# Turning 64-bit weights into float32: the exponent's shift of range moved into ScalarE's absolute value

## The chip, the cores and the metric

The kernel runs on one core of one Trainium2 chip. The core has TensorE (PE in the profile) for matrix products, VectorE (DVE), ScalarE (ACT), GpSimd (POOL) and SyncE (SP), whose queue issues most transfers. Each engine works through a queue of its own in order and waits on semaphores for the others. The metric is the device time of one execution in microseconds (us), from the median of several runs.

## What is computed

```python
# attention, per batch and head: x 512x64, state 32x64, in float32
xread = softmax(x @ state.T / 8) @ state
sread = softmax(state @ x.T / 8) @ x
# rows of both, concatenated: 4352 tokens of 512
...
h = x @ w_in                    # 512 -> 2048
g = np.maximum(h, 0.0) + np.log1p(np.exp(-np.abs(h)))
x = g @ w_out                   # 2048 -> 512
...
# a router gives every token to one of 8 experts, at most 544 each
out[mask] = np.maximum(x[mask] @ w1[e], 0.0) @ w2[e]
```

The weights `w_in` (512 x 2048) and `w_out` (2048 x 512) arrive as 64-bit floats. The chip's engines have no such type, so the kernel reads them as pairs of 32-bit integers, a low and a high word, and makes float32 numbers of them by bit operations. This is called turning the weights below.

## The kernel before

The program goes through attention and the first layer batch by batch (8 batches; the first product of the layer, then softplus, then the second product), then the routing, then the experts one after the other. Float32 products are made of three products of shorter parts: a matrix is split into `hi` (rounded, by ScalarE) and `lo` (what is left, by GpSimd or VectorE), and `hi*hi`, `hi*lo`, `lo*hi` are added up in PSUM.

The weights are turned while batch 0 is worked on. There are 32 units of 128 partitions x 512 numbers: 16 of `w_in` ("i") and 16 of `w_out` ("o"), in an order written out by hand (`queue`). A unit goes through these steps:

- `conv_load`: SyncE loads 512 KB of integers into a buffer `st64` (four of them).
- `conv_abs` (L181): ScalarE takes the absolute value of the high words, read as float32, into `c_a` (three of them).
- `conv_steps`, on VectorE: L196 raises it to at least 2^-15; L198 shifts it left by three and masks it; L200 joins sign and top exponent bit from the high word; L208 joins the three top bits of the low word, into `win` for an "i" unit, into a buffer `c_f` (four of them) for an "o" unit.
- `conv_post`, for an "o" unit: TensorE turns `c_f` (L232) into `p_bg`, ScalarE copies it to `wt` (L234) and rounds `c_f` into `wo_hi` (L238), and GpSimd makes `wo_lo` (L239).

`conv_steps` is a generator. Each `yield` ends a step, and `fill(n)`, called between other work, advances the units in progress by n steps; with two in progress it takes them in turn. A unit that ends starts the next load.

The work around it is written out by hand in rounds, one for each of the 16 column blocks `ft` of batch 0, as words in the strings `play0`; for the last seven rounds (9 to 15):

```python
play0 += ["g main main fill4 first a p att fill2 abs log abs second post fill2"] * 7
```

`first` is the first product of round s+2 (L493, six matmuls into `p_h`), `a` and `log` are ScalarE's parts of softplus (`t_sp`, L528, L535, L536), `g` is VectorE's sum for round s+1 (L548) with ScalarE's `g_hi` (L556) and GpSimd's `g_lo` (L559), and `second` is the second product (L577 with `wo_hi`, L579 with `wo_lo`, L581 with `g_lo`; twelve matmuls). `p` makes a pair `P_hi`, `P_lo` from `win` (L441 on TensorE, L427 on ScalarE, L429 on VectorE, with `fill(2)` between), and `att` is one step of the attention of the next batch (L386, L388, L334 and others on VectorE). `main` takes a unit into progress, `abs` is `conv_abs`, `post` is `conv_post`. The PSUM banks `bg0` and `bg1` are shared by all small products; a product into one of them waits until the last reader has finished.

Of the kernel before, what the change touches and what calls it, by code (L numbers as in the profile page):

```python
# [8 lines left out]
F32 = mybir.dt.float32  # L9
# [3 lines left out]
AF = mybir.ActivationFunctionType  # L13
OP = mybir.AluOpType
# [9 lines left out]
NJ4 = -(-NJ // 4) * 4  # L24
NFT = FF // 128
BIG = 3.0e38
TINY = 2.0 ** -15


@with_exitstack  # L30
def attn_moe_kernel(ctx, tc, x_s, x_t, state_t, w_in, w_out, w_gate, w1, w2, out):
    nc = tc.nc
    V, A, G, PE, SP = nc.vector, nc.scalar, nc.gpsimd, nc.tensor, nc.sync
# [141 lines left out]
    def conv_abs():  # L175
        if not loaded or len(ready) == 2:
            return
        u, st = loaded.pop(0)
        w = st.rearrange("p (n two) -> p n two", two=2)
        a = cv.tile([128, 512], F32, name="c_a", bufs=3)  # L180
        A.activation(a, w[:, :, 1].bitcast(F32), AF.Abs)  # L181
        ready.append((u, w[:, :, 0], w[:, :, 1], a))

    cops = []
# [1 line left out]
    def conv_main(n=1):  # L186

        for _ in range(n):
            if ready and not (ready[0][0][0] == "o" and len(turned) + sum(c[0] == "o" for c in cops) == 4):
                u, lo, hi, a = ready.pop(0)  # L190
                f = cv.tile([128, 512], F32, name="c_f", bufs=4) if u[0] == "o" else None
                cops.append((u[0], conv_steps(u, lo, hi, a, f)))

    def conv_steps(u, lo, hi, a, f):
        t = a.bitcast(I32)
        V.tensor_scalar(a, a, TINY, None, op0=OP.max)  # L196
        yield
        V.tensor_scalar(t, t, 3, 0x3FFFFFFF, op0=OP.logical_shift_left, op1=OP.bitwise_and)  # L198
        yield
        V.scalar_tensor_tensor(t, hi, -(1 << 30), t, op0=OP.bitwise_and, op1=OP.bitwise_or)  # L200
        yield
        if u[0] == "o":
            dst = f.bitcast(I32)
            turned.append((f, u[1]))
        else:
            dst = win[:, 2 * u[2]:2 * u[2] + 2, u[1] * 256:(u[1] + 1) * 256].bitcast(I32)
            lo, t = (x.rearrange("p (h c) -> p h c", h=2) for x in (lo, t))
        V.scalar_tensor_tensor(dst, lo, 29, t, op0=OP.logical_shift_right, op1=OP.bitwise_or)  # L208
# [487 lines left out]
    def play(script, s):  # L696
        for w in script.split():
            op, n = w.rstrip("0123456789"), w.lstrip("abcdefghijklmnopqrstuvwxyz")
            if op == "fill":
                fill(int(n))  # L700
            elif op == "att":
                if s < 0 or s in ATT0:
                    att_step(0)
            elif op == "first":
                mlp1(s + 2)
            elif op == "a":
                softplus_abs(s + 2)
            elif op == "g":
                softplus_b(s + 1)
            elif op == "second":  # L710
                mlp2(s)
                ghl.pop(s)
            else:
                {"main": conv_main, "abs": conv_abs, "post": conv_post, "p": p_unit, "log": softplus_log}[op]()
# [552 lines left out]
    for ph in range(E):  # L1267
# [19 lines left out]
        for u in range(16):  # L1287
            ft, hf = units[u] if ph else units0[u]
            f, c = slice(ft * 128, (ft + 1) * 128), HALF[hf]
            w = c.stop - c.start  # L1290
# [115 lines left out]
```

## Time and profile before

| | |
|---|---|
| median of 3 runs | 1197.72 us (1197.44 to 1198.61) |
| the profiled execution's own time | 1192.96 us |
| its span, first to last instruction | 1191.2 us |
| TensorE busy | 1137.9 us, 96% of the span |
| VectorE busy | 654.8 us, 55% |
| ScalarE busy | 640.1 us, 54% |
| GpSimd busy | 485.5 us, 41% |
| mean granted TensorE clock | 0.990 |

Busy time counts an instruction from start to end; matmuls overlap, so a busy TensorE is not one at its peak. The shares are means over stages that differ much from each other. The profiled execution is one run and not the median one, so durations read from it add up to its own time.

### The profile page before, as it was taken

The page shows a single profiled execution, that of the slowest core. Times are in us where ns is not written, and L with a number is a line of the kernel's source. Part 1 is how long each engine was busy: PE and PEld are TensorE (multiplying, and loading weights), DVE is VectorE, ACT ScalarE, POOL GpSimd, SP SyncE. Part 2 cuts the span into 40 slices and gives each one's busy share as a digit, 9 for nine tenths or more (in the row PEclk, how much of TensorE's full clock was granted, in tenths as well). Part 3 has the DMA queues.
Part 4 walks back from the last instruction along what each step waited for, and adds up shares of the span by engine and source line. Part 5 has one row for each costly group of instructions (what it writes and reads, how often), then busy time and mean ns, then how long its engine had stood idle before and what let it go on. Part 6 is the DMA issues. An engine that isn't in the chain of part 4 may idle for free.

```text
span 1191.2 us, 21162 instructions
## 1 busy us (share of the span) xinstructions
PE 1137.9 (96%) x8216; PEld 901.5 (76%) x8216; DVE 654.8 (55%) x1754; ACT 640.1 (54%) x1277; POOL 485.5 (41%) x472
## 2 busy tenths in 40 slices
PE   4898999999999999999999997999999999999996
PEld 1666677777777777777777765979797989889895
DVE  6999536463363533634434267776686858662220
ACT  3776666666676666766776732533333333334340
POOL 0334323233233232323344435645636555547531
PEclk9999999999999999999999999899999999999998
DMA  7464020111201102002000003250523324365401
GB/s 248 143 196 141 1 72 36 54 53 37 71 1 48 60 32 60 16 37 71 1 18 19 1 18 125 92 199 21 207 80 139 126 101 153 103 165 169 129 10 37
DMA packets 56020, 97.99 MB, mean 82 GB/s; under 512 B 5232, under 2 KB 24048, under 8 KB 55920
## 3 DMA queue, kind: packets, MB, share of 16 engines
q1 hardware_dynamic: 50192, 78.69, 20.6%
q0 software_dynamic: 5632, 17.83, 4.4%
q8 instruction: 64, 1.05, 0.4%
q14 instruction: 36, 0.29, 0.1%
q10 hardware_dynamic: 96, 0.13, 0.0%
HBM read 76.58 MB, written 17.83 MB: 79 GB/s over the span
## 4 chain that ended last, share of the span: by engine, by line
PE 80%; DVE 9%; issue 6%; POOL 2%; ACT 1%; DMA 1%; SPq 0%; POOLq 0%; DVEq 0%; ACTq 0%
PE p_h L493 13%; PE p_y L1344 12%; PE p_y L577 9%; PE p_y L579 8%; PE p_y L581 8%; PE p_y L1299 7%; PE p_h L1299 6%; PE p_bg L462 2%; PE p_y L584 2%; PE p_bg L504 2%; PE p_y L588 2%; PE p_y L586 2%; DVE c_a L200 1%; PE p_h L1208 1%; PE p_bg L1047 1%
## 5 line engine op out<-in xcount | busy, mean ns | idle before, releaser
L559 POOL TENSOR_TENSOR g_lo<-g,g_hi 128x512 fp32r<-128x512 f32 x127 | 164.8, 1298 | 318.3 <-ACT g_hi L556 287.5
L577 PE MATMUL p_y<-g_hi,wo_hi 128*128 128x512 f32 x448 | 184.5, 412 | 0.0
L579 PE MATMUL p_y<-g_hi,wo_lo 128*128 128x512 f32 x448 | 176.3, 393 | 3.4 <-POOL wo_lo L239 3.4
L581 PE MATMUL p_y<-g_lo,wo_hi 128*128 128x512 f32 x448 | 176.7, 394 | 0.6 <-POOL g_lo L559 0.6
L556 ACT ACTIVATE g_hi<-g 128x512 fp32r<-128x512 f32 x126 | 79.6, 631 | 115.3 <-DVE g L548 81.2
L548 DVE SCALAR_TENSOR_TENSOR g<-p_h,t_sp 128x512 f32<-128x512 f32 x128 | 87.5, 684 | 98.0 <-ACT t_sp L536 97.3
L577 PEld LDWEIGHTS p_y<-g_hi,wo_hi 128*128 128x128 f32 x448 | 84.8, 189 | 47.5 <-ACT t_sp L528 12.6
L1344 PE MATMUL p_y<-w2h,h2h 128*128 128x512 f32 x256 | 104.1, 406 | 0.0
L493 PE MATMUL p_h<-at_hi,P_hi 128*128 128x512 f32 x256 | 103.1, 403 | 0.0
L1344 PE MATMUL p_y<-w2l,h2h 128*128 128x512 f32 x256 | 101.4, 396 | 0.0
L1344 PE MATMUL p_y<-w2h,h2l 128*128 128x512 f32 x256 | 101.1, 395 | 0.0
L493 PE MATMUL p_h<-at_hi,P_lo 128*128 128x512 f32 x256 | 100.8, 394 | 0.0
L493 PE MATMUL p_h<-at_lo,P_hi 128*128 128x512 f32 x256 | 100.8, 394 | 0.0
L579 PEld LDWEIGHTS p_y<-g_hi,wo_lo 128*128 128x128 f32 x448 | 85.1, 190 | 20.2 <-POOL wo_lo L239 4.6
L581 PEld LDWEIGHTS p_y<-g_lo,wo_hi 128*128 128x128 f32 x448 | 84.7, 189 | 19.7 <-POOL g_lo L559 1.0
L1352 POOL DMA_INDIRECT out_dram<-ot,idx x40 | 38.8, 970 | 136.6 <-ACT ot L1333 69.2
L528 ACT ACTIVATE t_sp<-p_h 128x512 f32<-128x512 f32 x128 | 75.4, 589 | 25.5 <-PE p_h L493 25.5
L1178 POOL TENSOR_TENSOR w2l<-s2w,w2h 128x512 fp32r<-128x512 f32 x64 | 81.7, 1294 | 13.0 <-ACT w2h L1177 12.2
L1178 POOL TENSOR_TENSOR w1l<-s1w,w1h 128x512 fp32r<-128x512 f32 x63 | 80.2, 1300 | 7.8 <-ACT w1h L1177 7.3
L536 ACT ACTIVATE t_sp<-t_sp 128x512 f32<-128x512 f32 x128 | 81.0, 633 | 4.1
L535 ACT ACTIVATE t_sp<-t_sp 128x512 f32<-128x512 f32 x128 | 80.8, 631 | 2.3
L1299 PE MATMUL p_y<-yTl,w1h 128*128 128x288 f32 (+1 forms) x256 | 77.3, 302 | 0.0
(283 smaller groups left out, 2607.7 us busy)
## 6 DMA issues: line engine op xcount, KB each, us to landing
s2w<-in_moe_w_dram SPq DMA_DIRECT2D x8, 2048.0 KB, 9.4
s1w<-in_moe_w_dram SPq DMA_DIRECT2D x6, 2048.0 KB, 8.3
st<-in_moe_w_in_dram SPq DMA_DIRECT2D x16, 512.0 KB, 4.1
xT<-in_x_t_dram SPq DMA_DIRECT2D x16, 512.0 KB, 4.4
st<-in_moe_w_out_dram SPq DMA_DIRECT2D x16, 512.0 KB, 3.5
xt<-in_x_s_dram SPq DMA_DIRECT2D x8, 1024.0 KB, 5.5
y_d<-yz SPq DMA_DIRECT2D x48, 128.0 KB, 3.4
s1w<-in_moe_w_dram SPq DMA_DIRECT2D x8, 512.0 KB, 8.2
```

The source lines that it names most:

```text
L493: PE.matmul(h, l[:, f0:f0 + 128], r[:, par, :], start=(n == 0), stop=(n == 5))
L535: A.activation(t, t, AF.Exp, scale=-1.0)
L536: A.activation(t, t, AF.Ln, bias=1.0)
L548: V.scalar_tensor_tensor(g[:, :w], hps.pop(s)[:, :w], 0.0, tsp.pop(s)[:, :w], op0=OP.max, op1=OP.add)
L556: A.activation(hi[:, c], g[:, c], AF.Copy)
L559: (G if on[1] == "G" else V).tensor_tensor(lo[:, c], g[:, c], hi[:, c].bitcast(F32), op=OP.subtract)
L577: PE.matmul(yb[j], wo_hi[:, ft, c], hi, start=st, stop=False)
L579: PE.matmul(yb[j], wo_lo[:, ft, c], hi, start=False, stop=False)
L581: PE.matmul(yb[j], wo_hi[:, ft, c], lo, start=False, stop=sp)
L1178: eng.tensor_tensor(lo, src, hi.bitcast(F32), op=OP.subtract)
L1299: PE.matmul(p[:, :w], l[:, k, f], r[:, k, c], start=(n == 0), stop=(n == 11))
L1344: PE.matmul(p, l[:, ft, c], r[:, ft, :], start=(n == 0), stop=(n == 23))
```

## The change

The constant 2^-15 goes, and 2^-112 comes. ScalarE's absolute value multiplies by it: a float32's exponent field goes down by 112, so the bits that L198's mask cut off are already zero, and small numbers go to zero by themselves. VectorE's maximum (L196) is left out, and so is the mask of the shift (L198); the sign is now taken alone from the high word, without the exponent's top bit. A unit has three steps where it had four. Behind the edit, line numbers are two lower in the changed kernel: L198, L200 and L208 of before correspond to L196, L198 and L206.

```diff
--- before.py
+++ after.py
@@ -24,7 +24,7 @@
 NJ4 = -(-NJ // 4) * 4
 NFT = FF // 128
 BIG = 3.0e38
-TINY = 2.0 ** -15
+DOWN = 2.0 ** -112
 
 
 @with_exitstack
@@ -178,7 +178,7 @@
         u, st = loaded.pop(0)
         w = st.rearrange("p (n two) -> p n two", two=2)
         a = cv.tile([128, 512], F32, name="c_a", bufs=3)
-        A.activation(a, w[:, :, 1].bitcast(F32), AF.Abs)
+        A.activation(a, w[:, :, 1].bitcast(F32), AF.Abs, scale=DOWN)
         ready.append((u, w[:, :, 0], w[:, :, 1], a))
 
     cops = []
@@ -193,11 +193,9 @@
 
     def conv_steps(u, lo, hi, a, f):
         t = a.bitcast(I32)
-        V.tensor_scalar(a, a, TINY, None, op0=OP.max)
+        V.tensor_scalar(t, t, 3, None, op0=OP.logical_shift_left)
         yield
-        V.tensor_scalar(t, t, 3, 0x3FFFFFFF, op0=OP.logical_shift_left, op1=OP.bitwise_and)
-        yield
-        V.scalar_tensor_tensor(t, hi, -(1 << 30), t, op0=OP.bitwise_and, op1=OP.bitwise_or)
+        V.scalar_tensor_tensor(t, hi, -(1 << 31), t, op0=OP.bitwise_and, op1=OP.bitwise_or)
         yield
         if u[0] == "o":
             dst = f.bitcast(I32)
```

The instructions of TensorE, ScalarE, GpSimd and SyncE are the same and stand in the same order as before. On VectorE, fewer steps for the same `fill` calls change the order too. Two places are shown. In the rows, `c_a` and `st` are the unit in progress, `win` or `c_f` its result, numbers are buffers.

The first is VectorE's queue ahead of the first `g`, near 30 us; before:

```order
L429 TENSOR_TENSOR P_lo<-p_bg_275,P_hi 128x256
L200 SCALAR_TENSOR_TENSOR c_a<-st_204,c_a 128x512
L196 TENSOR_SCALAR c_a<-c_a 128x512
L429 TENSOR_TENSOR P_lo<-p_bg_289,P_hi 128x256
L208 SCALAR_TENSOR_TENSOR win<-st_204,c_a 128x2x256
L196 TENSOR_SCALAR c_a<-c_a 128x512
L198 TENSOR_SCALAR c_a<-c_a 128x512 x2
L548 SCALAR_TENSOR_TENSOR g<-p_h,t_sp 128x512
L200 SCALAR_TENSOR_TENSOR c_a<-st_208,c_a 128x512
L200 SCALAR_TENSOR_TENSOR c_a<-st_242,c_a 128x512
```

and now:

```order
L427 TENSOR_TENSOR P_lo<-p_bg_269,P_hi 128x256
L206 SCALAR_TENSOR_TENSOR win<-st_198,c_a 128x2x256
L196 TENSOR_SCALAR c_a<-c_a 128x512
L427 TENSOR_TENSOR P_lo<-p_bg_283,P_hi 128x256
L198 SCALAR_TENSOR_TENSOR c_a<-st_202,c_a 128x512
L196 TENSOR_SCALAR c_a<-c_a 128x512
L206 SCALAR_TENSOR_TENSOR c_f<-st_202,c_a 128x512
L198 SCALAR_TENSOR_TENSOR c_a<-st_236,c_a 128x512
L546 SCALAR_TENSOR_TENSOR g<-p_h,t_sp 128x512
L206 SCALAR_TENSOR_TENSOR win<-st_236,c_a 128x2x256
```

The first `g` had two joins from a unit's last two lines ahead of it in this piece, and now has four, of three units; the joins that stood behind it moved ahead.

The second is VectorE's queue in round 10, near 109 us, from the two units in progress there to the next `g`; before:

```order
L196 TENSOR_SCALAR c_a<-c_a 128x512 x2
L198 TENSOR_SCALAR c_a<-c_a 128x512 x2
L200 SCALAR_TENSOR_TENSOR c_a<-st_1121,c_a 128x512
L200 SCALAR_TENSOR_TENSOR c_a<-st_1128,c_a 128x512
L429 TENSOR_TENSOR P_lo<-p_bg_1261,P_hi 128x256
L448 COPY Vp<-p_bg_1261 128x8
L386 TENSOR_REDUCE m_1296<-p_bg_1291 128x16
L388 TENSOR_TENSOR P_994<-p_bg_1291,m_1296 128x512
L208 SCALAR_TENSOR_TENSOR c_f<-st_1121,c_a 128x512
L208 SCALAR_TENSOR_TENSOR c_f<-st_1128,c_a 128x512
L548 SCALAR_TENSOR_TENSOR g<-p_h,t_sp 128x512
```

and now:

```order
L196 TENSOR_SCALAR c_a<-c_a 128x512 x2
L198 SCALAR_TENSOR_TENSOR c_a<-st_1092,c_a 128x512
L198 SCALAR_TENSOR_TENSOR c_a<-st_1101,c_a 128x512
L206 SCALAR_TENSOR_TENSOR c_f<-st_1092,c_a 128x512
L206 SCALAR_TENSOR_TENSOR c_f<-st_1101,c_a 128x512
L427 TENSOR_TENSOR P_lo<-p_bg_1232,P_hi 128x256
L446 COPY Vp<-p_bg_1232 128x8
L384 TENSOR_REDUCE m_1267<-p_bg_1262 128x16
L386 TENSOR_TENSOR P_971<-p_bg_1262,m_1267 128x512
L546 SCALAR_TENSOR_TENSOR g<-p_h,t_sp 128x512
```

The two last joins of the units, into `c_f`, moved from behind the attention step (L386, L388, now L384, L386) to ahead of `P_lo`, and two shifts are gone.

## Rows read from the trace of the kernel before

**Rows 1.** The page: engines, then two groups of ScalarE instructions (count, busy us, mean ns).

```profile
PE 1137.9 (96%) x8216; PEld 901.5 (76%) x8216; DVE 654.8 (55%) x1754; ACT 640.1 (54%) x1277; POOL 485.5 (41%) x472
...
L536 ACT ACTIVATE t_sp<-t_sp 128x512 f32<-128x512 f32 x128 | 81.0, 633 | 4.1
L535 ACT ACTIVATE t_sp<-t_sp 128x512 f32<-128x512 f32 x128 | 80.8, 631 | 2.3
```

**Rows 2.** Windows: stretch, its length, engines' busy us (instructions), granted clock, DMA share, GB/s.

```profile
0.00:37.40 37.40, 19.61 (x131) 10.30 (x131) 27.47 (x57) 17.29 (x31) 2.51 (x8) 1.00 0.68 226
37.40:119.72 82.32, 73.19 (x779) 50.98 (x777) 75.69 (x136) 57.53 (x111) 33.26 (x24) 0.96 0.49 161
119.72:145.68 25.96, 24.29 (x260) 17.38 (x257) 13.64 (x29) 17.50 (x35) 9.69 (x8) 1.00 0.01 2
145.68:1191.20 1045.52, 1020.87 (x7064) 822.79 (x7055) 537.96 (x1534) 547.77 (x1102) 440.01 (x435) 0.99 0.23 73
```

**Rows 3.** Groups of instructions by line from 37.40 to 119.72 us.

```profile
L559 POOL TENSOR_TENSOR g_lo<-g,g_hi 128x512 fp32r<-128x512 f32 x13 | 17.6, 1355 | 27.3 <-ACT g_hi L556 27.3
...
L239 POOL TENSOR_TENSOR wo_lo<-c_f,wo_hi 128x512 fp32r<-128x512 f32 x11 | 17.3, 1574 | 23.4 <-ACT wo_hi L238 23.4
...
L198 DVE TENSOR_SCALAR c_a<-c_a 128x512 int32<-128x512 int32 x23 | 12.5, 560 | 0.2
```

**Rows 4.** TensorE in order of time: start, duration; the round starts that are used.

```profile
37.40 0.47 PE L577 MATMUL p_y<-g_hi,wo_hi 128*128 128x512 f32 x1
...
103.42 0.50 PE L577 MATMUL p_y<-g_hi,wo_hi 128*128 128x512 f32 x1
...
109.55 0.48 PE L577 MATMUL p_y<-g_hi,wo_hi 128*128 128x512 f32 x1
...
119.72 0.48 PE L577 MATMUL p_y<-g_hi,wo_hi 128*128 128x512 f32 x1
```

**Rows 5.** TensorE in order of time: matmuls that waited, idle time and releaser in brackets.

```profile
51.52 0.62 PE L441 MATMUL p_bg<-win,stT 64*32 64x256 f32 x4 [1.87 <-DVE win L208]
...
76.01 0.63 PE L232 MATMUL p_bg<-ident,c_f 128*128 128x128 f32 x4 [0.63 <-DVE sr L334]
...
81.36 0.50 PE L579 MATMUL p_y<-g_hi,wo_lo 128*128 128x512 f32 x1 [0.49 <-POOL wo_lo L239]
...
95.81 0.62 PE L441 MATMUL p_bg<-win,stT 64*32 64x256 f32 x4 [1.55 <-DVE win L208]
...
112.23 0.61 PE L579 MATMUL p_y<-g_hi,wo_lo 128*128 128x512 f32 x1 [2.20 <-POOL wo_lo L239]
```

**Rows 6.** VectorE and GpSimd in order of time, at two places.

```profile
77.27 1.29 POOL L559 TENSOR_TENSOR g_lo<-g,g_hi 128x512 fp32r<-128x512 f32 x1 [5.26 <-ACT g_hi L556]
77.91 1.20 DVE L208 SCALAR_TENSOR_TENSOR c_f<-st,c_a 128x512 int32<-128x512 int32 x1
...
107.23 0.68 DVE L208 SCALAR_TENSOR_TENSOR c_f<-st,c_a 128x512 int32<-128x512 int32 x1
...
109.10 0.75 DVE L198 TENSOR_SCALAR c_a<-c_a 128x512 int32<-128x512 int32 x2
109.11 3.07 POOL L239 TENSOR_TENSOR wo_lo<-c_f,wo_hi 128x512 fp32r<-128x512 f32 x1 [4.63 <-ACT wo_hi L238]
109.77 1.28 DVE L200 SCALAR_TENSOR_TENSOR c_a<-st,c_a 128x512 int32<-128x512 int32 x2
110.98 0.41 DVE L429 TENSOR_TENSOR P_lo<-p_bg,P_hi 128x256 fp32r<-128x256 f32 x1
...
112.09 0.69 DVE L388 TENSOR_TENSOR P<-p_bg,m 128x512 f32<-128x512 f32 x1
```

**Rows 7.** Windows: two stretches with a lower granted clock.

```profile
82.00:84.00 2.00, 2.00 (x6) 1.54 (x5) 1.97 (x6) 0.45 (x1) 0.00 (x0) 0.50 0.68 184
112.00:116.00 4.00, 3.77 (x10) 2.95 (x11) 3.90 (x7) 1.21 (x2) 1.42 (x2) 0.57 0.43 165
```

**Rows 8.** VectorE in order of time: the first `g`.

```profile
33.58 0.68 DVE L548 SCALAR_TENSOR_TENSOR g<-p_h,t_sp 128x512 f32<-128x512 f32 x1
```

## The prediction

> **What bounds the kernel now.** I read the page first, then the windows that cut the span into stages, then TensorE's order of time in the stage that the change touches, and last VectorE and GpSimd side by side there.
>
> Over the whole span TensorE is busy 96% and VectorE 55% [rows 1], so an average says that VectorE work is free. The windows say otherwise for the stretch in which the weights are turned [rows 2]. From 37.40 to 119.72 us VectorE is busy 75.69 of 82.32 us, while TensorE is idle 82.32 - 73.19 = 9.13 us and its clock has a mean of 0.96. After that stretch, from 119.72 to 145.68, VectorE falls to 13.64 of 25.96 us and TensorE idles 1.67. After 145.68 neither line of the change runs any more: whatever the stage saves or costs moves the rest of the program as a whole, and TensorE is busy there 1020.87 of 1045.52 us.
>
> The stage is made of rounds, one for each `ft` of batch 0. TensorE starts the second product of round 0 at 37.40 and that of round 11 at 119.72 [rows 4], so eleven rounds take 82.32 us, 7.48 each. Round 9 to 10 shows what a round takes when nothing is late: 109.55 - 103.42 = 6.13 us. What is late elsewhere stands in TensorE's own waits [rows 5]: 1.87 us for `win` from VectorE, 0.63 for `sr`, 0.49 for GpSimd's `wo_lo`, 1.55 for `win` again, 2.20 for `wo_lo`. Three of the five wait straight for the VectorE queue.
>
> The 2.20 needs the two engines side by side [rows 6]. GpSimd's `g_lo` runs from 77.27 to 78.56; VectorE's L208, issued at 77.91, takes 1.20 us instead of 0.68, so its 0.6 of work begins when GpSimd ends. At 109.11 it is the other way: `wo_lo` takes 3.07 us instead of 1.29, while two L198 and two L200 run on VectorE until 111.05. The two engines take turns at these instructions. Their undisturbed need in the stage is 23 units of 2 x 0.335 + 2 x 0.60 = 1.87 us on VectorE (steps: two L198 from 109.10 to 109.77, two L200 from there to L429 at 110.98; L208 is taken like L200, having 0.68 alone), that is 43.0 us, and 24 GpSimd instructions of 1.29, that is 31.0. Together 74.0 us of 82.32: 90% [rows 2, 3, 6]. This taking of turns bounds the stage, more than either engine alone.
>
> The Trainium skill (SBUF — State Buffer, "Who interferes with whom") says the same as an exclusive lock: VectorE in a two-port mode, or with two SBUF inputs, against a GpSimd instruction that reads SBUF. These rows agree; its further rule, that issue order decides who blocks, is the third rival below.
>
> **The change, part by part.**
>
> *The scale on L181.* 32 ScalarE instructions stay, with a factor in them. L535 carries a factor of -1 and takes 631 ns, L536 carries none and takes 633 [rows 1]: I add 0. From below a gain is excluded, since nothing is taken out; from above the bound is the spread between those two rows, under 0.01 us each, 0.3 us for 32.
>
> *The two VectorE steps become one.* L196 (a maximum, float32) and L198 (shift and mask, int32) go; a shift alone on int32 comes, as the new L196. It is not in the trace. L196 with one operation and L198 with two are alike when undisturbed, and L198's step is 0.335 us [rows 6], so one operation on int32 should be that too; I take 0.335. The dear end is L200's 0.605 per step, the cheap end 0.335, since no row here shows 512 elements in less. L200's constant changes from -2^30 to -2^31: nothing.
>
> So every one of the 32 units loses one step of 0.335 us, 23 of them in the stage [rows 3]: 23 x 0.335 = 7.7 us. In busy time L198 has 12.5 us there, 560 ns each; the difference is waiting for GpSimd inside the instruction, and that wait passes on to the next one, so I don't count it. Cross-check by turns: 74.0 - 7.7 = 66.3 us, at the same 90%, is 73.7 us instead of 82.3: -8.6. Both say about -8.
>
> *The clock.* The granted clock is 0.50 from 82 to 84 us and 0.57 from 112 to 116 [rows 7], the lower of TensorE's two levels for most of it; the first comes soon after the wait at 81.36, the second on the 2.20 us wait [rows 5]. A mean of 0.96 over 82.32 us costs 0.04 x 82.32 = 3.3 us of TensorE's speed. With less idle time ahead of them some of these drops should go; I take half, -1.6, with 0 and -3.3 as ends.
>
> The Trainium skill (TensorE: Matmul & The Clock Gate, "What's actually happening") says that the clock is full only while the array is kept busy; by that alone both drops would go and the whole 3.3 us come back. No row here tells how much idle time it takes, so half it stays.
>
> *The order.* `fill(n)` advances the conversions by n steps wherever it stands, and a unit now has three steps instead of four, so the same `fill` calls finish units sooner, and other VectorE work stands behind them. In round 10 the two L208 into `c_f` come ahead of `P_lo` and of L386/L388, where they stood behind them. The second of these needs a `c_f` buffer that GpSimd's `wo_lo` must free. Behind it wait `P_lo` (the next round's `p_bg`) and L388, and for L388 TensorE's turn L232. L388 ended at 112.78 before [rows 6]; with 0.67 us less of L198 and 1.2 us more of L208 ahead of it, it comes 0.5 us later. L232 stands behind the twelve matmuls of the second product, which began at 109.55, so most of that is hidden; the cover would be gone, and the 0.5 paid in full, if L208 also waited for `wo_lo`. In other rounds the same shift puts one L208 (0.60) ahead of `P_lo`, less one L198 or more. I take +0.8 us for the stage, from 0 to 11 x 0.60 = 6.6.
>
> *The start.* Before 37.40 nine units are turned, so nine steps, 3.0 us, go at most. But the chain runs through the first `g` (L548 at 33.58) [rows 8], on which the bank of the third first product hangs. Three more of the 0.605 us steps now stand ahead of it, 1.8 us, against eight steps gone (the first unit's is not on the way), 2.7: 0.9 earlier at most by VectorE's queue. Also the loads that feed units one to three land when they land: the windows show 226 GB/s and a DMA share of 0.68 over that stretch [rows 2]. I take -0.5, from 0 to -3.0.
>
> *After the stage.* From 119.72 on, the waits are not for conversions: 0.
>
> Sum: -7.7 - 1.6 + 0.8 - 0.5 = -9.0 us. Against the profiled execution's own time, 1192.96 us (span 1191.2 and 1.8 around it), that is 1184.0; the runs shown have a median of 1197.72, 4.8 above that execution, and the same -9.0 on the median gives 1188.7 us (-0.75%). A measurement of this kernel can tell about 0.2%, 2.4 us, from no change.
>
> **The rivals.**
>
> *TensorE becomes the bound at once.* All of its idle time in the stage and all lost clock come back: -9.13 - 3.3 - 0.5 = -12.9, 1184.8 us. For it: rounds of 6.13 exist already. Against it: the turns with GpSimd would still take 66.3 us of the 69.9 left, 95%, and ScalarE's 57.53 us sit beside them.
>
> *The gain is hidden by ScalarE and loads.* `t_sp`, `g`, `g_hi`, `g_lo` follow one another across three engines; if this chain sets the round, a shorter conversion only waits longer for `c_a`. Then only the waits straight on `win` go, in part: half of 1.87 + 1.55, and the start's 0.5: -2.2, 1195.5 us. Against it: ScalarE is busy 57.53 of 82.32 us [rows 2], and round 9 to 10 ran in 6.13 us with ScalarE's full work in it.
>
> *GpSimd is shut out.* The other side. L200 and L208 now follow each other with no shift between; if GpSimd loses its turn as it did at 109.11, `wo_lo` and so L579 come late. The price is one more L208 pair, 1.2 us, in each of eleven rounds: +13.2 - 7.7 = +5.5, 1203.2 us. It decides from 7.7 / 11 = 0.7 us a round. Against it: in the same trace `g_lo` at 77.27 kept its 1.29 us, with an L208 waiting, and VectorE gives up 7.7 us of turns.
>
> By the skill's rule on issue order this could fall either way, since it depends on which of the two is issued first in each round; this is the 0.07.
>
> *The shift is not fast.* At 0.605 a step, the gain falls to 23 x 0.065 = 1.5, and with the start 2.0: 1195.7 us. Against it: L198 shifts int32 by the same count at 0.335.
>
> **How the numbers follow.** Forecast 0.60; TensorE at once 0.12; hidden 0.13; GpSimd shut out 0.07; slow shift 0.08. The forecast's own range is 1185.0 to 1192.5. For 8 in 10 the range takes in the TensorE rival below and most of the hidden one above: 1183.0 (the clock's and start's full ends, -14.7) to 1196.0. Faster by over 0.2% means under 1195.3: 0.60 + 0.12 + half of the hidden case and some of the slow shift, 0.82. Slower is the GpSimd rival, 0.07. The rest, 0.11, is within 0.2%.
>
> **What would show it.** The new L196 at about 0.43 us alone and 0.335 a step, 32 of them, and L181 no dearer than before. Round 0 to round 11 in about 74 us instead of 82.32, TensorE idle in it about 3 us, no 3.07 us `wo_lo`. The start of round 0 at about 36.9. The stretch behind the stage as long as before, within 1 us. I am wrong if rounds keep 7.5 us with VectorE idle in them (then ScalarE or the loads bound them), or if `wo_lo` is stretched in most rounds.

## The result, and the profile after

The changed kernel takes 1188.51 us (median of 6 runs, 1187.83 to 1189.78), before 1197.67 (6 runs); the ratio is 0.9915, with a 95% interval of 0.9904 to 0.9926. That is 9.2 us less, against 9.0 forecast. Its profiled execution took 1188.37 us, with a span of 1186.6.

The windows of the kernel after, cut at the starts of rounds 0, 11 and 16 (16 is the first round behind batch 0; columns as in [rows 2]):

```profile
0.00:37.22 37.22, 18.02 (x131) 9.20 (x131) 25.65 (x50) 18.05 (x32) 3.32 (x8) 1.00 0.74 244
37.22:111.47 74.25, 70.25 (x778) 49.75 (x777) 67.48 (x111) 56.82 (x111) 31.82 (x23) 0.97 0.52 169
111.47:142.40 30.93, 30.11 (x281) 22.27 (x279) 14.96 (x35) 19.98 (x40) 10.12 (x8) 0.95 0.00 1
142.40:1186.60 1044.20, 1017.09 (x7036) 819.02 (x7034) 535.43 (x1529) 544.69 (x1097) 438.73 (x433) 0.99 0.23 73
```

and those of the kernel before behind round 11, cut at the start of round 16 too:

```profile
119.72:150.36 30.64, 28.96 (x282) 21.17 (x279) 16.35 (x35) 20.24 (x41) 11.20 (x9) 1.00 0.01 1
150.36:1191.20 1040.84, 1016.19 (x7036) 819.01 (x7034) 535.25 (x1529) 545.03 (x1097) 438.49 (x433) 0.99 0.23 73
```

The start is 0.2 us shorter (37.22 against 37.40). Rounds 0 to 11 take 74.25 us instead of 82.32 [rows 2]: 8.07 us, nearly all of the gain, and VectorE is busy 8.2 us less in them. Rounds 11 to 16 take 30.93 instead of 30.64. So round 16 starts 7.96 us earlier. Behind it this trace is 3.4 us longer (1044.20 against 1040.84), which is why the two spans differ by 4.6 only. Part of it is seen as a wait that no engine releases, at one place of the experts' stage that the change doesn't touch:

```profile
943.21 0.43 PE L1328 MATMUL p_y<-s2w,h2t 128*32 128x128 f32 x6 [1.03 <-issue]
```

In the changed kernel's other trace (below) the stretch behind round 16 takes 1041.9 us, so this belongs to the one execution, and not to the change. The profiled execution of before was a short one too, 4.7 us under the median of its runs. With the second traces of both kernels (below), round 16 starts at 150.36 and 153.04 us before, and at 142.40 and 142.26 now: a gain of 8.0 to 10.8 us, in which the 9.2 of the medians lies.

The groups of the stage from 37.22 to 111.47 that answer to [rows 3], and the new L196 in order of time, twice undisturbed and once beside GpSimd:

```profile
L198 DVE SCALAR_TENSOR_TENSOR c_a<-st,c_a 128x512 int32<-128x512 int32 x23 | 21.8, 965 | 0.2
...
L557 POOL TENSOR_TENSOR g_lo<-g,g_hi 128x512 fp32r<-128x512 f32 x12 | 17.1, 1421 | 19.7 <-ACT g_hi L554 19.7
...
L237 POOL TENSOR_TENSOR wo_lo<-c_f,wo_hi 128x512 fp32r<-128x512 f32 x11 | 14.9, 1351 | 22.6 <-ACT wo_hi L236 21.1 <-PE p_h L491 1.6
...
L196 DVE TENSOR_SCALAR c_a<-c_a 128x512 int32<-128x512 int32 x23 | 13.9, 624 | 3.4 <-ACT c_a L181 3.4
```

```profile
42.80 0.75 DVE L196 TENSOR_SCALAR c_a<-c_a 128x512 int32<-128x512 int32 x2
...
84.02 0.42 DVE L196 TENSOR_SCALAR c_a<-c_a 128x512 int32<-128x512 int32 x1
...
93.54 1.29 DVE L196 TENSOR_SCALAR c_a<-c_a 128x512 int32<-128x512 int32 x2
```

The new shift takes 0.42 us alone and 0.75 us for two, as its forerunner L198 did (0.75 in [rows 6]), and 624 ns in the mean: VectorE still waits for GpSimd inside it. `wo_lo` has a mean of 1351 ns instead of 1574, and no instance of 3.07 us.

What is not better in this trace is round 10. TensorE in order of time:

```profile
37.22 0.47 PE L575 MATMUL p_y<-g_hi,wo_hi 128*128 128x512 f32 x1
...
100.67 0.48 PE L575 MATMUL p_y<-g_hi,wo_hi 128*128 128x512 f32 x1
...
106.49 0.63 PE L230 MATMUL p_bg<-ident,c_f 128*128 128x128 f32 x4 [2.84 <-DVE P L386]
...
111.47 0.78 PE L575 MATMUL p_y<-g_hi,wo_hi 128*128 128x512 f32 x1
```

It takes 10.80 us (10.17 before [rows 4]), with a new wait, 2.84 us for L386. The queue of VectorE and GpSimd ahead of it shows why:

```profile
99.27 1.84 DVE L196 TENSOR_SCALAR c_a<-c_a 128x512 int32<-128x512 int32 x2
99.53 1.29 POOL L237 TENSOR_TENSOR wo_lo<-c_f,wo_hi 128x512 fp32r<-128x512 f32 x1 [3.55 <-ACT wo_hi L236]
100.78 1.48 POOL L557 TENSOR_TENSOR g_lo<-g,g_hi 128x512 fp32r<-128x512 f32 x1
101.03 2.38 DVE L198 SCALAR_TENSOR_TENSOR c_a<-st,c_a 128x512 int32<-128x512 int32 x2
103.33 1.28 DVE L206 SCALAR_TENSOR_TENSOR c_f<-st,c_a 128x512 int32<-128x512 int32 x2
104.53 0.41 DVE L427 TENSOR_TENSOR P_lo<-p_bg,P_hi 128x256 fp32r<-128x256 f32 x1
...
105.65 0.69 DVE L386 TENSOR_TENSOR P<-p_bg,m 128x512 f32<-128x512 f32 x1
```

Both GpSimd instructions run while VectorE's L196 and L198 are due, which take turns with them: the pairs are stretched to 1.84 and 2.38 us. L206 then stands ahead of L386, as the order of the change put it, and L386 ends at 106.34, 5.67 us behind the start of the round's second product (3.23 before). TensorE has idled for 2.84 us when it goes on at 106.49. In this trace the granted clock falls behind the wait, to a mean between its lower level (0.50 in [rows 7]) and the full one:

```profile
106.00:112.00 6.00, 5.51 (x55) 3.73 (x56) 4.10 (x7) 4.43 (x9) 2.51 (x2) 0.63 0.01 3
```

### The profile page after: what moved, and what is told of

Its sections match the earlier page's. It is cut to its first block, busy times and chain, and to the rows that moved or that the text cites. A ratio compares the mean times of both kernels' runs of the same rounds, so it can differ in the third digit from the quotient of the medians.

```text
span 1186.6 us, 21131 instructions
## 1 busy us (share of the span) xinstructions
PE 1135.5 (96%) x8216; PEld 900.2 (76%) x8216; DVE 643.5 (54%) x1722; ACT 639.5 (54%) x1277; POOL 484.0 (41%) x472
## 4 chain that ended last, share of the span: by engine, by line
PE 77%; DVE 9%; issue 6%; ACT 3%; POOL 2%; DMA 1%; SPq 1%; another core or an unknown queue 0%; POOLq 0%; DVEq 0%; ACTq 0%
PE p_h L491 13%; PE p_y L1342 11%; PE p_y L575 8%; PE p_y L579 8%; PE p_y L577 8%; PE p_y L1297 7%; PE p_h L1297 6%; PE p_bg L460 2%; PE p_y L582 2%; PE p_bg L502 2%; PE p_y L586 2%; PE p_y L584 2%; PE p_h L1206 1%; DVE c_a L198 1%; PE p_bg L1045 1%
```

## The experiments

The ratios below are against before on the same chip, where before had medians of 1195.36 to 1195.46 us.

**The kernel before again.** No edit.

> The kernel of before once more, as a measure of what two equal programs differ by, and for a second trace of it. Its first profiled execution took 1192.96 us, 4.7 less than its median of 1197.67. If that difference lies in the rounds that turn the weights, rounds 0 to 11 take about 87 us here instead of 82.3; if it lies behind them, they take 82.3 again, and the time shows up as waits of TensorE that no engine releases (the rows call them issue). The time itself: 1197.6, ratio 1.000.

Ratio 1.0000 (0.9991 to 1.0009); 1195.37 us. Its rounds 0 to 11, and what lies behind round 16:

```profile
37.65:122.55 84.90, 75.66 (x779) 52.98 (x777) 75.52 (x136) 57.85 (x112) 33.11 (x24) 0.92 0.48 156
153.04:1194.80 1041.76, 1017.00 (x7036) 819.56 (x7034) 535.15 (x1529) 545.13 (x1097) 438.12 (x433) 0.99 0.23 73
```

Behind round 16 it takes 1041.76 us, within 1 us of the first trace; the rounds take 84.90 instead of 82.32. So most of the spread of before lies in the rounds (2.6 of the 3.6 us between the two spans), as the first half of the expectation had it, though by less. VectorE's busy time is the same (75.52 against 75.69); the clock is not: 0.92 against 0.96, which is 0.08 x 84.90 = 6.8 us of TensorE's speed against 3.3.

**The order alone.**

```diff
         V.tensor_scalar(a, a, TINY, None, op0=OP.max)
-        yield
         V.tensor_scalar(t, t, 3, 0x3FFFFFFF, op0=OP.logical_shift_left, op1=OP.bitwise_and)
```

> Before's arithmetic (maximum, then shift and mask) in the changed kernel's order: the first two instructions of a unit form one step. Theory A (a step's worth of turns between VectorE and GpSimd was removed, and the order costs a little): 0.8 to 4 us slower than before, 1198.5 to 1201.5. Rival B (the gain comes from the order, units finish sooner): about 1190.

Ratio 1.0043 (1.0029 to 1.0056), 1201.69 us: slower, so the order makes none of the gain, and by itself it costs about 5 us, more than the 4 expected at most. Two of TensorE's long waits in it, and the start of round 0 between them:

```profile
38.49 0.50 PE L492 MATMUL p_h<-at_hi,P_hi 128*128 128x512 f32 x1 [2.43 <-DVE g L547]
...
43.17 0.78 PE L576 MATMUL p_y<-g_hi,wo_hi 128*128 128x512 f32 x1
...
124.84 0.87 PE L231 MATMUL p_bg<-ident,c_f 128*128 128x128 f32 x3 [3.58 <-DVE P L387]
```

Round 0 begins 5.8 us later than before, behind a wait for the first `g`, and round 10 has its wait for the attention step, 3.58 us. These 5 us are the order's price with before's arithmetic; the next run shows that it is less with the new one.

**The work alone.**

```diff
         V.tensor_scalar(t, t, 3, None, op0=OP.logical_shift_left)
         yield
+        yield
```

> The changed kernel's arithmetic in before's order: the second step of a unit is empty. Theory A: faster than the changed kernel by what its order costs. The changed kernel's trace has a wait of 2.84 us for L386 in round 10 and a half clock behind it; if both go, 1184.5 to 1186.5. If the order costs nothing, 1188.5. Rival B (the order makes the gain): 1196 or more.

Ratio 0.9911 (0.9895 to 0.9927), 1183.91 us: the whole gain is there in before's order. Theory A had expected 2 to 4 us more than that. They did not come: 0.9911 differs from the changed kernel's 0.9915 (0.9918 in its second set) by less than the intervals, 0.5 to 0.8 us, though the wait for L386 is gone. So with the new arithmetic the order costs nothing that can be told from noise. The rounds, and TensorE in round 10:

```profile
35.28:109.73 74.45, 70.68 (x778) 49.83 (x777) 66.62 (x113) 57.87 (x112) 33.37 (x24) 0.98 0.55 178
```

```profile
102.28 0.48 PE L576 MATMUL p_y<-g_hi,wo_hi 128*128 128x512 f32 x1
...
103.83 0.50 PE L578 MATMUL p_y<-g_hi,wo_lo 128*128 128x512 f32 x1 [1.07 <-POOL wo_lo L238]
```

Round 0 starts at 35.28, 1.9 us ahead of the changed kernel. Up to round 10 the rounds take 102.28 - 35.28 = 67.00 us, where the changed kernel took 100.67 - 37.22 = 63.45; round 10 takes 109.73 - 102.28 = 7.45, where that took 10.80. So the new order gives 3.6 us in ten rounds, and gives more than that back at the start (1.9) and in round 10 (3.4). Part of the 3.6 is work that the new order does ahead of round 0: VectorE has 103 instructions in these ten rounds here, and 99 in the changed kernel. The kernel that has before's order in the start alone (below) takes 65.49 us for them: by these single traces about 2 of the 3.6 come from the order in the start, and 1.5 from that in the rounds.

**A reduction in the removed step's place.**

```diff
+        d = cv.tile([128, 1], F32, name="c_d", bufs=1)
+        V.tensor_reduce(d, a[:, 0:256], axis=AX, op=OP.max)
+        yield
         V.tensor_scalar(t, t, 3, None, op0=OP.logical_shift_left)
         yield
```

> The changed kernel, with a maximum over 256 numbers of c_a into a one-column tile (its result is used nowhere) where before had its first step, so before's order and about before's VectorE time (0.335 us a step by the reduction of 512, less 256 elements), but in an instruction that by the Trainium skill (SBUF, State Buffer, Who interferes with whom) doesn't take turns with GpSimd. Theory A (the turns bound the rounds): within 2.5 us of the kernel with the changed arithmetic in before's order, so 1185 to 1190. Rival C (VectorE's queue alone bounds the rounds, turns or not): the whole gain is lost, 1196 to 1198.

Ratio 0.9997 (0.9988 to 1.0006), 1195.02 us: the whole gain is lost. The rounds, the reduction's group in them, and all 32 reductions (shortest, median and longest, ns):

```profile
38.83:120.41 81.58, 72.94 (x779) 51.33 (x777) 75.42 (x135) 57.01 (x111) 30.34 (x22) 0.96 0.49 162
```

```profile
L197 DVE TENSOR_REDUCE c_d<-c_a 128x1 f32<-128x256 f32 x23 | 9.4, 411 | 2.1 <-ACT c_a L181 1.7
```

```profile
L197 DVE TENSOR_REDUCE c_d<-c_a x32: 400/410/420, 5.7 to 118.7; 128x1 f32<-128x256 f32 x32
```

23 reductions of 411 ns give VectorE its busy time back (75.42 us, 75.69 before) and the rounds their length (81.58, 82.32). Theory A, that the turns with GpSimd are what bounds them, falls; rival C, VectorE's queue, stands. That these reductions take no turns is seen in their times: the longest of 32 took 420 ns, while the shift behind them (L199 here) had a mean of 700 in the rounds. The trace of before has it too, at two L404 (a reduction of 1024 numbers), one beside GpSimd's `g_lo` and one beside nothing:

```profile
52.87 1.36 POOL L559 TENSOR_TENSOR g_lo<-g,g_hi 128x512 fp32r<-128x512 f32 x1 [3.15 <-ACT g_hi L556]
52.99 1.20 DVE L404 TENSOR_REDUCE m<-ST 128x2 f32<-128x1024 f32 x1
...
134.83 1.21 DVE L404 TENSOR_REDUCE m<-ST 128x2 f32<-128x1024 f32 x1
```

Both last 1.2 us. The Trainium skill (SBUF — State Buffer, "Who interferes with whom") says that a reduction never contends with GpSimd, and the rows agree.

**GpSimd's work doubled.**

```diff
         (G if on[1] == "G" else V).tensor_tensor(lo[:, c], g[:, c], hi[:, c].bitcast(F32), op=OP.subtract)
+        if s < NFT:
+            j = cv.tile([128, 256], BF, name="c_j", bufs=1)
+            for h in (0, 256):
+                G.tensor_tensor(j, g[:, h:h + 256], hi[:, h:h + 256].bitcast(F32), op=OP.subtract)
```

> The changed kernel, in which GpSimd makes every g_lo of batch 0 a second time behind the first, in two halves into a tile that nobody reads: some 1.4 us more of GpSimd's time in each of 14 rounds, off its own queue's needs. Theory C (VectorE's queue sets the rounds, and what GpSimd holds adds to it where they meet): VectorE has something to do in most of that time, half of it lies over instructions that wait: +5 to +10 us. Theory D (VectorE's queue sets the rounds, and turns cost next to nothing): within 2 us of the changed kernel. Theory A of the earlier set (the turns alone bound the rounds, 1.4 us each): +14 to +18.

Ratio 1.0005 (0.9996 to 1.0015), 1196.17 us, against 0.9918 for the changed kernel in the same set: 0.0087 x 1195.4 = 10.4 us. The rounds, and the added group in them:

```profile
37.81:120.16 82.35, 73.33 (x778) 50.85 (x777) 76.80 (x109) 56.12 (x108) 55.71 (x46) 0.96 0.45 148
```

```profile
L561 POOL TENSOR_TENSOR c_j<-g,g_hi 128x256 bf16<-128x256 f32 x23 | 24.7, 1072 | 0.9
```

Not one VectorE instruction was added, and VectorE is busy 76.80 us instead of 67.48, and the rounds take 82.35 instead of 74.25. GpSimd's 24.7 us more cost 8.1 in the rounds, a third of themselves (10.1 against the changed kernel's second trace): theory C, a little above what it expected. Not all of it came through VectorE. GpSimd's own queue makes `wo_lo` later too, and TensorE waits for it three times in these rounds, 2.74 us together, where the changed kernel has 0.23:

```profile
80.14 0.50 PE L581 MATMUL p_y<-g_hi,wo_lo 128*128 128x512 f32 x1 [1.42 <-POOL wo_lo L237]
...
87.29 0.50 PE L581 MATMUL p_y<-g_hi,wo_lo 128*128 128x512 f32 x1 [0.74 <-POOL wo_lo L237]
...
94.25 0.50 PE L581 MATMUL p_y<-g_hi,wo_lo 128*128 128x512 f32 x1 [0.58 <-POOL wo_lo L237]
```

Together the last two say what the prediction had wrong: the turns are not the bound, they are a part of VectorE's time.

**The attention step first again.**

```diff
-play0 += ["g main main fill4 first a p att fill2 abs log abs second post fill2"] * 7
+play0 += ["g main main fill2 first a p att fill2 abs log abs second post fill2"] * 7
```

> The changed kernel with fill2 in place of fill4 in the last seven rounds' string, which puts P_lo and the attention step (L384, L386) ahead of the units' last two instructions again in rounds 9 and 10. Theory A (in the changed kernel the units' ends ahead of L386 cost round 10 its 2.84 us wait and a half clock): round 10 falls from 10.80 us to about 7.5, and the time is 2.5 to 4 us under that of the changed kernel in this set. Rival B (round 10 is long for another reason, since it took 10.17 before and 11.39 in the other trace of before): no change, within 1 us of the changed kernel.

Ratio 0.9903 (0.9886 to 0.9920), 1183.01 us, 2.0 under the changed kernel of the set, a little less than expected; the two intervals overlap. Rounds 0 to 11, and 11 to 16:

```profile
36.84:107.99 71.15, 68.77 (x779) 48.95 (x777) 64.48 (x111) 56.43 (x110) 31.66 (x23) 1.00 0.53 176
107.99:138.67 30.68, 29.00 (x281) 21.17 (x280) 16.36 (x35) 20.24 (x41) 11.21 (x9) 1.00 0.01 1
```

Round 11 follows after 71.15 us instead of 74.25 (72.21 in the second trace of the changed kernel), round 10 takes 107.99 - 100.39 = 7.60, as theory A expected, and the wait for L386 is gone. The mean clock is 1.00 in both stretches. That the lower clock went because the wait went is not shown: the second trace of the changed kernel (below) has the same wait with the full clock behind it.

**And before's order in the start.**

```diff
         V.tensor_scalar(t, t, 3, None, op0=OP.logical_shift_left)
         yield
+        if turn_of[1]:
+            yield
```

> As att_first, and the empty second step until the first round, which gives the start before's order. Theory A (the start's order is why the changed kernel's start gained only 0.2 us, where the kernel with before's order throughout began round 0 at 35.28 instead of 37.22): round 0 begins at about 35.3, the rounds take what they take in att_first, and the time is 1.5 to 2.5 us under att_first, 4 to 6 under the changed kernel. Rival B (what the start gains, the rounds lose, since they wait for VectorE anyway): the time of att_first.

Ratio 0.9884 (0.9869 to 0.9900), 1181.43 us: the fastest of the full kernels, and faster than the changed kernel in the set (0.9903 at least). Against att_first the intervals overlap. TensorE's start of round 0, and its first wait behind it:

```profile
35.78 0.48 PE L577 MATMUL p_y<-g_hi,wo_hi 128*128 128x512 f32 x1
...
41.74 0.64 PE L441 MATMUL p_bg<-win,stT 64*32 64x256 f32 x8 [1.31 <-DVE Vp L448]
```

Round 0 starts 1.1 us earlier than in att_first, and loses 1.31 us to a wait in round 0: its round 11 starts at 108.85, 0.9 us later than there. In the trace rival B is right, and that the median is 1.6 us lower is not explained by it.

**The changed kernel again.** No edit.

> The changed kernel again, beside its variants on one chip, and for a second trace. 0.9915 of before as measured, about 10 us. If its round 10 takes 10 us or more again and its time behind the rounds is within 1 us of the first trace's, the differences of the variants can be read round by round.

Ratio 0.9918 (0.9903 to 0.9933), 1185.00 us, the first result again. Round 0 starts at 39.11 us in its trace, later than in the first, rounds 0 to 11 take 72.21, and round 16 starts at 142.26, as there (142.40). Round 10, 9.07 us, has the same wait, and behind it the clock stays full. TensorE's wait, and windows of the 8 us behind it:

```profile
108.03 0.63 PE L230 MATMUL p_bg<-ident,c_f 128*128 128x128 f32 x4 [2.79 <-DVE P L386]
```

```profile
108.00:112.00 4.00, 3.97 (x57) 2.96 (x58) 2.10 (x4) 3.97 (x9) 1.81 (x2) 1.00 0.02 4
112.00:116.00 4.00, 3.19 (x17) 2.42 (x16) 3.90 (x8) 1.45 (x3) 0.72 (x1) 1.00 0.00 0
```

Neither of the two conditions was met: round 10 takes less than 10 us, and the time behind round 16, 1041.94 us, is 2.3 under that of the first trace. So two traces of one kernel differ by some 2 us in a stage, and differences of that size between single traces of the variants don't show an effect.

**VectorE's next step left out.** The sign's join is dropped from att_first; its `yield` stays.

```diff
-        V.scalar_tensor_tensor(t, hi, -(1 << 31), t, op0=OP.bitwise_and, op1=OP.bitwise_or)
         yield
```

> att_first with the sign's join (L198) left out, its step left empty, so the weights lose their signs and the output is another; 0.60 us less of VectorE per unit in before's terms, 13.9 us over the 23 units of the rounds. Theory C (VectorE's queue still sets the rounds after the change): another 5 us or more under att_first, down to where TensorE alone sets them: its shortest rounds, 5.7 us and the attention's matmuls on top, make about 67 us of rounds 0 to 11 where att_first took 71.2, and the start gains 1 to 3. Rival D (TensorE and ScalarE set the rounds already in att_first, VectorE is out of the way): within 2 us of att_first, 0.9903 of before.

Ratio 0.9830 (0.9816 to 0.9843), 1175.08 us, 7.9 under att_first (8.7 by the ratios, since the two were measured on different chips). The rounds:

```profile
35.03:102.41 67.38, 66.87 (x779) 48.72 (x777) 49.14 (x88) 57.68 (x112) 30.87 (x24) 1.00 0.57 186
```

67.38 us, the 67 expected of TensorE alone: it is busy 66.87 of them, VectorE 49.14. So with the attention step first VectorE still sets the rounds, and some 4 of their 71.15 us are left to gain.

## Why the prediction was right, and where it was off

The sum said -9.0 us, the runs -9.2. Its terms:

- **The scale on ScalarE at 0: right.** The 32 instances of L181 take 671 ns in the mean, 677 before, and the order of ScalarE's work is the same; the whole gain is there with the scale in (the work alone).
- **One step of 0.335 us in 23 units, 7.7 us: right in size.** The rounds are 8.07 shorter, and 7.87 with the work alone (74.45), against the first trace of before; against its second they are 10 to 13 shorter. The shift is as fast as forecast.
- **Why it counts: wrong.** "This taking of turns bounds the stage, more than either engine alone" is refuted by the reduction, which brought the time back without a turn. What the rounds follow is VectorE's busy time, its waits for GpSimd included:

| kernel | VectorE busy in rounds 0 to 11 | rounds 0 to 11 | mean clock |
|---|---|---|---|
| before | 75.69 | 82.32 | 0.96 |
| before, second trace | 75.52 | 84.90 | 0.92 |
| order alone | 78.22 | 86.35 | 0.90 |
| reduction in its place | 75.42 | 81.58 | 0.96 |
| GpSimd doubled | 76.80 | 82.35 | 0.96 |
| changed | 67.48 | 74.25 | 0.97 |
| changed, second trace | 63.74 | 72.21 | 0.98 |
| work alone | 66.62 | 74.45 | 0.98 |
| attention step first | 64.48 | 71.15 | 1.00 |
| and before's order in the start | 66.40 | 73.07 | 1.00 |
| sign left out | 49.14 | 67.38 | 1.00 |

  In the first ten the difference is 5.6 to 9.4 us; in the last, TensorE has taken over. VectorE's time is not all of it, as the two traces of before show. The cross-check by turns gave nearly the same, -8.6, since the removed step is taken off by both ways of counting.
- **The clock, -1.6: not settled.** In the first trace of the changed kernel the mean is 0.97 over 74.25 us and 0.95 over the next 30.93, so 2.2 + 1.5 = 3.7 us of TensorE's speed are lost; in the second it is 0.98 over 72.21 and 1.00 behind, 1.4 us. Before lost 3.3 in one trace and 6.8 in the other. By these pairs the term lies between +0.4 and -5.4.
- **The order, +0.8: right in size by the medians, by luck.** The changed kernel is 0.5 to 0.8 us behind the work alone, within noise. The working behind it was off: its place and mechanism were named, the units' ends ahead of L386 and the cover of the second product, but L386 came 2.4 us later against the start of the round's second product, not 0.5, and the cover went entirely, a wait of 2.84 us. What the same order gives in rounds 0 to 10, 3.6 us with the start's part in it, I had not seen.
- **The start, -0.5: not settled.** It was -0.2 in one trace and +1.7 in the other (39.11), whose rounds were 2.0 us shorter for it; without the order's change it was -2.1 (35.28), most of the 3.0 that the prediction had as an end.

So the sum is right in more than its total: without the order's term it says -9.8, and the work alone gave 10.6 us (0.9911 of 1195.4). Luck is in the order's term: losses in the start and in round 10 and a gain in the other rounds, neither of them foreseen in size, come to about the +0.8 that was taken. The low end of the range, 1183.0, is not the sum that stands beside it: 7.7, with the full ends of clock and start, 3.3 and 3.0, makes -14.0 and not -14.7. Of the rivals, TensorE at once is what is left when another VectorE step goes, and "GpSimd is shut out" did not come: the longest `wo_lo` in the trace is 1.62 us, against 3.07 in [rows 6].

The Trainium skill (SBUF — State Buffer, "Who interferes with whom") says that VectorE in a two-port mode and GpSimd hold the shared ports for a whole instruction, and that the other waits. Of an instruction with two SBUF inputs, like L198, it says that it contends. The trace of the changed kernel shows the same whole wait there: two L198 in round 10 took 2.38 us instead of 1.28, and the first of them, begun at 101.03, ended at 102.81, 0.55 us behind the end of `g_lo` (102.26).

Open: what made the first trace of the changed kernel 2 to 3 us longer behind round 16 than all others (the 1.03 us wait is a part), and why the kernel with before's order in the start has a median 1.6 us under that with the attention step first alone, while its trace is 1.4 us longer. Open too is how much of GpSimd's price comes through VectorE, and how much through its own late `wo_lo`.

## What to carry to other kernels

An engine that is busy 55% of the span may be the bound of one stage; cut the span into windows by the other engine's rounds before an edit is called free. To tell which resource an instruction costs, put one of the same length but another kind in its place: here the time came back, so it was the queue. And where steps are dealt out by count, fewer steps per unit also move work: check what now stands ahead of the instruction that the other engine asks for next. Take a second trace of both kernels before a difference of 2 us in a stage is called an effect: here the clock and a round's length changed by that much with no edit.

## What was not expected of the hardware

Equal work on VectorE can leave TensorE with different time: the two traces of before have 75.69 and 75.52 us of VectorE in rounds 0 to 11, and clocks of 0.96 and 0.92. The same wait can leave TensorE with a different clock: 2.84 us of idling had 0.63 of the full clock behind it in one trace of the changed kernel (106 to 112 us), and 2.79 us had 1.00 in the other. And what two engines do to each other goes both ways: GpSimd's added halves took 1072 ns in the mean in the rounds, and 742 from 126 to 146 us, where VectorE has less to do:

```profile
L561 POOL TENSOR_TENSOR c_j<-g,g_hi 128x256 bf16<-128x256 f32 x6 | 4.5, 742 | 0.2
```
